# Second half of an adaLN modulation: from TensorE in the projection stage to GpSimd in the attention stage

## The chip, the cores and the metric

The kernel runs on one core of a Trainium2 chip. The metric is the device time of one execution in microseconds (us). Five engines take part, each with its own queue of instructions that it works off in order: PE (matmuls, with PEld for its weight loads), DVE (VectorE), ACT (ScalarE), POOL (GpSimd) and SP, whose queue issues nearly all DMAs. An instruction that waits holds up everything behind it on its engine.

## The reference, cut to what matters

A transformer block on 2048 tokens of width 448, all in fp32: the conditioning vector `c` gives six rows of modulation, then attention with 16 heads of 28, then an MLP of width 1792.

```python
mod = (silu(c) @ w_mod).reshape(1, 6, 1, 448)
sa, ca, ga, sb, cb, gb = (mod[:, i] for i in range(6))
h = layernorm(x) * (1 + ca) + sa
x = x + ga * attention(h, wqkv, wo)          # softmax over all 2048 keys
h = layernorm(x) * (1 + cb) + sb
x = x + gb * mlp(layernorm(h), w1, b1, w2, b2)   # gelu
```

`sa` and `ca` are needed at once. `ga`, `sb`, `cb` and `gb` come into play late: `ga` is multiplied into the rows of `wo`, `gb` into `w2` and `b2`, `sb` and `cb` make the input of the MLP.

## The kernel before, in words

The work has three stages, and all of its order is written out by hand: each engine's queue is the order in which the Python code emits instructions.

**Projection (0 to 166 us).** The tokens are in four blocks `b` of 512. For each block a list of tasks is run through, numbered `n`: products of queries or keys for one group of four heads (`qk_task`), products of values (`v_task`). A task is 11 matmuls into a PSUM tile `pa`. Between tasks PE is given maxima: the softmax needs the maximum of each query's scores, and it is found ahead by a product of one key chunk with one query chunk into a PSUM tile of a ring of five (`ma`, `ma`, `m`, `m`, `m`; line 476) and a reduction by DVE into a small tile `mxp` (line 481). Some maxima go in pairs: ACT takes the relu of a difference (L489), DVE finishes it in a custom instruction (L493). Into the first four tasks of block 1 the second part of the modulation is put, `mod_mm(0)` to `mod_mm(3)`: each multiplies `silu(c)` (128 x 32 weights, `sil_b`) with 128 rows of `w_mod` (1792 columns, loaded by `mod_load` into `slot_v`) in four matmuls that write 32 partitions each of one tile `o` (L752). `mod_fin` copies the sums out with ACT, writes them to DRAM (`drow`) and reads each of the four rows back, spread over 128 partitions.

**Attention (166 to 794 us).** 16 units (four groups of heads times four query blocks), 16 steps each, 256 steps. In a step PE makes the scores of one key chunk for four heads in two halves (L1382, tiles `s`), ACT takes their exponential (L1395), and PE multiplies those of the step before with the values (L1337, tile `o`). Maxima for later units are put between. Up to step 120 three PSUM tiles (`m`) are there for them; from step 121 (`RING`) one of these banks becomes a third `s` tile, a single tile `m` is left for single maxima, and maxima in pairs go into the `s` tile that is free just then (L686). At the end of a unit `unit_end_tasks` divides by the softmax sums: a reciprocal on DVE, a trip through DRAM that spreads it, a product on POOL (`t_split`, L1062), a rounding to fp32r on DVE (`t_split2`, L1072), the remainder on POOL (L1073), and eight DMAs that store both. `max_fin` gathers a unit's maxima into a tile `m32`, whose unused half POOL zeroes each time (L517). Tasks that belong to a certain step are put into a table by `at(step, fn)` and run at the end of that step. So is the preparation of `wo` (five items: a product with `ga` on POOL, a rounding on DVE, L987, a remainder on POOL), from step 4 on.

**Projection by `wo` and MLP.** Units 12 and 13 (steps 216 to 219 and 232 to 235) hold the output projection of the first two query blocks, which needs `wo`. The MLP follows after step 255, 794 to 1097 us.

The tiles `slot_a2h`, `slot_a3h` and `slot_b1h` belong to weights and inputs in the projection stage. In the attention stage `b1h` is used in step 0, and all three take outputs of attention from step 205 on.

Of the kernel before, what the change touches and what calls it, by code (L numbers as in the profile page):

```python
# [22 lines left out]
D = 448  # L23
# [21 lines left out]
def tile_adaln_block(ctx: ExitStack, tc: tile.TileContext, x, wqkv, wo, w1, b1, w2, b2, c, w_mod, out):  # L45
# [75 lines left out]

    ident = sbt("ident", [128, 128])
    make_identity(nc, ident)
    cst = sbt("cst", [128, 5])
    neg_half, zero_col = cst[:, 0:4], cst[:, 4:5]
    pool.memset(neg_half, -0.5)
    pool.memset(zero_col, 0.0)


    cols = sbt("cols", [128, 2 * NC])  # L130
# [183 lines left out]
    pc = ps_o()  # L314
    pe.transpose(pc[:, :NC], c_rows, ident[:NC, :NC])
    act.activation(sil_b, pc[:, :NC, None].broadcast_to([128, NC, 32]), AF.Silu)
    warm_up(5)
    for k in range(NC):
        for j in range(2):
# [190 lines left out]
            at(clock[0] + 4, lambda: make_kd(g))  # L510

    late = []


    def max_fin(g, qt):
# [223 lines left out]

    mod = {}  # L740

    def mod_load(k):
        mod[k] = slot(f"v{2 + k % 2}", [128, 4 * D], F32)
        load_mod(mod[k], k, 2 * D, 4)

    def mod_mm(k):
        if k == 0:
            mod["p"] = ps_o()
        p = mod["p"]
        for j in range(4):  # L750
            rs_, cs = mod_part(k, j, 4)
            pe.matmul(  # L752
                p[32 * j : 32 * j + 32, :D], sil_b[rs_, k, :], mod[k][rs_, cs],
                start=(k == 0), stop=(k == NC - 1),
            )

    def mod_fin():
        t = sbt("full", [128, 512], bufs=3)
        act.copy(t[0:64, :D], mod["p"][0:64, :D])
        act.activation(t[64:96, :D], mod["p"][64:96, :D], AF.Identity, bias=1.0)  # L760
        act.copy(t[96:128, :D], mod["p"][96:128, :D])
# [56 lines left out]
    for b in range(NB):  # L818
# [12 lines left out]
        for n, (tb, kind, g) in enumerate(tasks):  # L831
# [130 lines left out]
    def wo_item(n):  # L962
# [11 lines left out]
        def go(r):  # L974
            full = sbt("full", [128, 512], bufs=3)
            ps = slice(0, 112 if n == 3 else 128)
            pool.tensor_tensor(out=full[ps, :D], in0=r[ps, :D], in1=rows["ga"][ps], op=ALU.mult)

            def rest():
                if n == 3:  # L980
                    hi = sbt("hi", [128, 512], F32R, bufs=3)
                    dve.tensor_copy(hi[ps, :D], full[ps, :D])
                    pool.tensor_tensor(out=wo_p[1][ps, 2, :], in0=full[ps, :D], in1=f(hi)[ps, :D], op=ALU.subtract)
                    pool.tensor_copy(wo_p[1][0:32, 2, :], f(hi)[0:32, :D])
                    return
                k = min(n, 3)
                dve.tensor_copy(wo_p[0][:, k, :], full[:, :D])  # L987
# [3 lines left out]
            at(6 + 2 * n, rest)  # L991

        return ld, go

# [44 lines left out]
    def unit_end_tasks(u, o_sb):  # L1039
# [24 lines left out]
        def t_split2():  # L1064
# [7 lines left out]
            (dve.tensor_copy if staged else act.copy)(hi, on)  # L1072
# [179 lines left out]
        sched.setdefault(step, []).append(fn)  # L1252

    wo_prep = Prep([wo_item(n) for n in range(5)])
    at(0, lambda: wo_prep.load(2))
    for n in range(5):
        at(4 + 2 * n, wo_prep.step)

    def b2_load():
        rows["b2"] = raw_t()  # L1260
# [13 lines left out]
        at(1 + i, lambda: put_spare(1))  # L1274
    for g in (1, 2):
        at(6 + g, lambda g=g: put_ones(g))
    at(15, b2_load)
    at(28, b2_mul)
    last0 = NKT * (NU - 1)
    lnst = [ln2_stages(b) for b in range(NB)]  # L1280
    for i in range(14):
# [259 lines left out]
```

## Time and profile before

| | |
|---|---|
| median of 3 runs | 1099.84 us (1099.55 to 1100.01) |
| profiled execution | 1099.75 us, span 1097.5 us |
| busy in the span | PE 1088.1 us, DVE 805.1, ACT 697.6, POOL 198.7 |
| granted TensorE clock | 1.00 throughout |
| HBM | 59.39 MB read, 29.50 MB written |

The span begins with the first instruction that was recorded; 2.25 us of the execution lie outside of it. In the timeline a row is one or more instructions of one line in a row: start, duration of the whole row, engine, line, operation, tiles written and read, shape, count, and in brackets the engine's idle time before it with what ended it. Matmuls overlap in PE's pipeline, so that a row of several is shorter than their sum; PEld rows mark the moments at which PE took up a matmul.

### The profile page before, as it was taken

How to read it: one execution, taken by the hardware profiler on the slowest of the kernel's cores; microseconds unless marked ns; L12 is line 12 of the kernel's file. 1: busy time of each engine (PE TensorE's matmuls, PEld its weight loads, DVE VectorE, ACT ScalarE, POOL GpSimd, SP SyncE). 2: the span in 40 equal slices, each digit the busy share in tenths (PEclk: the TensorE clock that was granted, in tenths of full speed). 3: DMA queues.
4: the chain of work that ended last, by engine and by line, in shares of the span. 5: the costliest groups of instructions: out<-in, count | busy, mean ns of one | idle time of the engine just before them, and what ended most of it. 6: DMA issues, size and time to landing. Idle time of an engine off the chain costs nothing.

```text
span 1097.5 us, 20709 instructions
## 1 busy us (share of the span) xinstructions
PE 1088.1 (99%) x8255; PEld 658.3 (60%) x8255; DVE 805.1 (73%) x1382; ACT 697.6 (64%) x883; POOL 198.7 (18%) x201
## 2 busy tenths in 40 slices
PE   8999999999999999999999999999999999999998
PEld 6756675444444444444444444554488788888887
DVE  6968788999999999988888888575655565463322
ACT  4565667888888888888888888678933411211211
POOL 1543332210000000000000000217123042061000
PEclk9999999999999999999999999999999999999999
DMA  9563354121222201232211213111442302002000
GB/s 312 207 190 103 97 188 134 59 65 32 72 76 64 77 28 41 67 98 54 69 48 38 86 49 104 58 31 59 136 137 65 101 34 55 18 34 72 34 1 34
DMA packets 58438, 88.57 MB, mean 81 GB/s; under 512 B 13759, under 2 KB 25686, under 8 KB 58330
## 3 DMA queue, kind: packets, MB, share of 16 engines
q1 hardware_dynamic: 57858, 86.51, 26.3%
q8 instruction: 65, 1.06, 0.4%
q10 hardware_dynamic: 148, 0.46, 0.1%
q0 software_dynamic: 336, 0.28, 0.1%
q14 instruction: 31, 0.25, 0.1%
HBM read 59.39 MB, written 29.50 MB: 81 GB/s over the span
## 4 chain that ended last, share of the span: by engine, by line
PE 96%; DVE 2%; DMA 1%; ACT 1%; issue 0%; SPq 0%; DVEq 0%; ACTq 0%
PE s L1382 23%; PE o L1337 23%; PE m L396 16%; PE pa L396 9%; PE m L476 8%; PE s L1472 3%; PE s L1473 3%; PE s L1474 3%; PE s L476 2%; PE t L1473 1%; PE t L1474 1%; PE t L1472 1%; DVE y L1193 1%; DMA slot_c<-in_w_mod_dram 1%; PE o L277 1%; DVE mxp L481 0%
## 5 line engine op out<-in xcount | busy, mean ns | idle before, releaser
L481 DVE TENSOR_REDUCE mxp<-m 128x1 f32<-128x512 f32 x555 | 359.7, 685 | 65.0 <-PE m L476 49.6
L1382 PE MATMUL s<-slot_b,slot_a 28*128 28x512 f32 (+1 forms) x3072 | 356.7, 423 | 0.0
L1382 PEld LDWEIGHTS s<-slot_b,slot_a 28*128 28x128 f32 (+1 forms) x3072 | 211.1, 183 | 176.0 <-ACT slot_c L1395 96.4
L476 PE MATMUL m<-kh,qh 28*128 28x512 f32 x607 | 226.9, 468 | 0.5 <-DVE mxp L481 0.3
L1395 ACT ACTIVATE slot_c<-s 128x1024 f32<-128x1024 f32 x170 | 174.7, 1028 | 51.6 <-PE s L1382 50.8
L1337 PE MATMUL o<-slot_c,v 128*32 128x512 f32 x680 | 178.9, 605 | 0.0
L1428 ACT ACTIVATE full<-m,b_col 128x512 f32<-128x512 f32 x56 | 38.6, 689 | 206.6 <-PE m L396 201.4
L686 DVE TENSOR_REDUCE mxp<-s 128x2 f32<-128x1024 f32 x107 | 131.1, 1226 | 5.1
L1337 PE MATMUL o<-slot_c1h,v 128*32 128x512 f32 x512 | 134.7, 605 | 0.0
L1337 PE MATMUL o<-slot_c0h,v 128*32 128x512 f32 x508 | 133.6, 605 | 0.0
L1395 ACT ACTIVATE slot_c1h<-s 128x1024 f32<-128x1024 f32 x128 | 130.7, 1021 | 0.0
L1395 ACT ACTIVATE slot_c0h<-s 128x1024 f32<-128x1024 f32 x127 | 130.5, 1028 | 0.0
L1395 ACT ACTIVATE slot_d<-s 128x1024 f32<-128x1024 f32 x86 | 88.4, 1028 | 25.0 <-PE s L1382 24.7
L1431 DVE CAST hi<-full 128x512 fp32r<-128x512 f32 x42 | 18.7, 444 | 112.3 <-ACT full L1428 112.3
L476 PEld LDWEIGHTS m<-kh,qh 28*128 28x128 f32 x607 | 90.7, 182 | 15.2 <-DVE mxp L481 13.1
L1337 PE MATMUL o<-slot_d,v 128*32 128x512 f32 x344 | 90.5, 605 | 0.4 <-ACT osb L1301 0.4
L1062 POOL TENSOR_TENSOR osb<-osb,osb 128x512 f32<-128x512 f32 x16 | 20.6, 1286 | 362.8 <-DMA osb<-drec 343.5
L1432 DVE TENSOR_TENSOR lo<-full,hi 128x512 fp32r<-128x512 f32 x56 | 46.0, 822 | 29.7 <-ACT hi L1431 25.1
L396 PE MATMUL m<-y,slot_a 128*128 128x512 f32 x160 | 60.9, 397 | 0.4 <-DVE y L1193 0.2
L481 DVE TENSOR_REDUCE mxp<-ma 128x1 f32<-128x512 f32 x61 | 39.5, 681 | 13.2 <-PE m L476 9.2
L1337 PEld LDWEIGHTS o<-slot_c,v 128*32 128x32 f32 x680 | 24.5, 108 | 39.1 <-issue 36.5
L650 DVE CUSTOM_DVE_ANT_0 slot_d0i<-m,slot_d0i 128x512 f32<-128x512 f32 x54 | 37.3, 691 | 14.3 <-PE m L476 11.3
(351 smaller groups left out, 1824.2 us busy)
## 6 DMA issues: line engine op xcount, KB each, us to landing
slot_b<-d SPq DMA_DIRECT2D x32, 256.0 KB
slot_a<-d SPq DMA_DIRECT2D x32, 256.0 KB
d<-lo SPq DMA_DIRECT2D x28, 256.0 KB
d<-hi SPq DMA_DIRECT2D x16, 256.0 KB
osb<-drec SPq DMA_DIRECT2D x15, 256.0 KB
out_dram<-xn SPq DMA_DIRECT2D x16, 224.0 KB
raw<-in_B_w_dram SPq DMA_DIRECT2D x14, 224.0 KB
qh<-d SPq DMA_DIRECT2D x12, 256.0 KB
```

Of the source, the lines that this page charges most:

```text
L396: pe.matmul(p, a, b, start=(i == 0), stop=(i == len(terms) - 1))
L476: pe.matmul(m, qh_sb[(g, qt)][js, i * 128 : (i + 1) * 128], k[js, :], start=True, stop=True)
L481: dve.tensor_reduce(out=mxp[(g, qt)][:, i, j, cch : cch + 1], in_=m, op=ALU.max, axis=AX.X)
L686: dve.tensor_reduce(out=mxp[(g, qt)][:, i, j : j + 2, cch], in_=t, op=ALU.max, axis=AX.X)
L1337: pe.matmul(o[32 * j : 32 * j + 32, :], v_sb[kt // 4][:, kt % 4, 4 * g + j, :], p[j // 2][:, j % 2, :], start=(kt == 0), stop=(kt == NKT - 1),
L1382: pe.matmul(s2[:, jj, :], ks[rows_, kp, kc], qs[rows_, qp, :], start=(term == 0), stop=(term == 2))
L1395: act.activation(pt[hf], s2, AF.Exp, scale=SCALE)
L1428: act.activation(gf, p, AF.Gelu_apprx_tanh, bias=b1_col[:, i : i + 1])
L1432: dve.tensor_tensor(out=glo, in0=gf, in1=f(ghi), op=ALU.subtract)
L1472: pe.matmul(pp, ghi[:, ts], w_hi, start=(m == 0), stop=False)
L1473: pe.matmul(pp, ghi[:, ts], w_lo, start=False, stop=False)
L1474: pe.matmul(pp, glo[:, ts], w_hi, start=False, stop=(m == NFT - 1))
```

## The change

Three things are done at once.

1. The second part of the modulation leaves PE and the projection stage. ACT makes `sil_c` (128 x 4) at the start. In steps 124 to 161 of attention, every fifth step, one chunk of `w_mod` (128 rows, or for the last of each half 64, by 896 columns) is loaded into `slot_a2h`; two steps later POOL multiplies it with a column of `sil_c` and adds it to a running sum (`slot_b1h` for `ga` and `sb`, `slot_a3h` for `cb` and `gb`). In step 166 four matmuls with a column of ones as weights (one that `v_sb` holds already) sum over the partitions, into the single tile `m`; one ACT instruction copies the result, with a bias column `third` that adds the 1 of `cb`.
2. With it, the preparation of `wo` moves from steps 4 to 14 to steps 178 to 188, the load of `b2` from 15 to 189 and its product from 28 to 202.
3. The rounding in `t_split2` goes to POOL where results are stored (units 0 to 11 and 14), and `m32` becomes two fixed tiles that are zeroed once.

The diff, without the constants' other uses:

```diff
+MOD_AT = 124
+WO_AT = 178
...
+    act.activation(sil_c, pc[:, :NC], AF.Silu)
...
-        m32 = sbt("m32", [128, 32], F32R, bufs=2)
-        pool.memset(f(m32)[:, 16:32], 0.0)
+        m32s.append(m32s.pop(0))
+        m32 = m32s[-1]
...
-    def mod_load(k):
-        mod[k] = slot(f"v{2 + k % 2}", [128, 4 * D], F32)
-        load_mod(mod[k], k, 2 * D, 4)
-
-    def mod_mm(k):
-        if k == 0:
-            mod["p"] = ps_o()
-        p = mod["p"]
+    def mod_load(h, k):
+        rs_ = mod_rows(h, k)
+        mod["raw"] = slot("a2h", [128, 2 * D], F32)
+        c0 = 2 * D * (1 + h)
+        sp.dma_start(mod["raw"][rs_], w_mod[128 * k : min(128 * k + 128, D), c0 : c0 + 2 * D])
+
+    def mod_add(h, k):
+        rs_ = mod_rows(h, k)
+        if k == 0:
+            mod[h] = slot(("b1h", "a3h")[h], [128, 2 * D], F32)
+        raw, total = mod["raw"][rs_], mod[h][rs_]
+        col = sil_c[rs_, k : k + 1].broadcast_to([rs_.stop - rs_.start, 2 * D])
+        pool.tensor_tensor(out=raw if k else total, in0=raw, in1=col, op=ALU.mult)
+        if k:
+            pool.tensor_tensor(out=total, in0=total, in1=raw, op=ALU.add)
+
+    def mod_fin():
+        p = ps_mx()
+        ones_ = v_sb[0].rearrange("p t h d -> p (t h) d")[:, 0:32, DH]
         for j in range(4):
-            rs_, cs = mod_part(k, j, 4)
             pe.matmul(
-                p[32 * j : 32 * j + 32, :D], sil_b[rs_, k, :], mod[k][rs_, cs],
-                start=(k == 0), stop=(k == NC - 1),
+                p[32 * j : 32 * j + 32, :D], ones_, mod[j // 2][:, j % 2 * D : (j % 2 + 1) * D], start=True, stop=True,
             )
-
-    def mod_fin():
         t = sbt("full", [128, 512], bufs=3)
-        act.copy(t[0:64, :D], mod["p"][0:64, :D])
-        act.activation(t[64:96, :D], mod["p"][64:96, :D], AF.Identity, bias=1.0)
-        act.copy(t[96:128, :D], mod["p"][96:128, :D])
+        act.activation(t[:, :D], p[:, :D], AF.Identity, bias=third)
...
-            if b == 0 and n == 6:
-                mod_load(0)
-                mod_load(1)
-            if b == 1:
-                if n < 2:
-                    mod_mm(n)
-                    mod_load(2 + n)
-                elif n in (2, 3):
-                    mod_mm(n)
-                    if n == 3:
-                        mod_fin()
...
-            (dve.tensor_copy if staged else act.copy)(hi, on)
+            (pool.tensor_copy if staged else act.copy)(hi, on)
...
-    at(0, lambda: wo_prep.load(2))
+    for i in range(2 * NC):
+        h, k = divmod(i, NC)
+        at(MOD_AT + 5 * i, lambda h=h, k=k: mod_load(h, k))
+        at(MOD_AT + 5 * i + 2, lambda h=h, k=k: mod_add(h, k))
+    at(MOD_AT + 10 * NC + 2, mod_fin)
+    at(WO_AT - 4, lambda: wo_prep.load(2))
     for n in range(5):
-        at(4 + 2 * n, wo_prep.step)
+        at(WO_AT + 2 * n, wo_prep.step)
```

PE's order at the end of the third task of block 1, in the kernel before (`ma` and `m` are the ring of tiles for maxima, `slot_v` holds `w_mod`, `pa` is the next task's tile):

```order
L476 MATMUL ma_847<-kh_162_730,qh_60_323 128x512
L476 MATMUL m_191_850<-kh_162_730,qh_60_323 128x512
L476 MATMUL m_192_853<-kh_162_730,qh_60_323 128x512
L476 MATMUL m_193_856<-kh_74_361,qh_158_708 128x512
L752 MATMUL o_761<-slot_v_172_766,slot_d_4_86 32x448 x4
L396 MATMUL pa_876<-slot_c_110_510,slot_a_20_125 128x512
L396 MATMUL pa_876<-slot_c_110_510,slot_a_22_127 128x512
```

The same place in the changed kernel:

```order
L481 MATMUL ma_836<-kh_163_733,qh_63_330 128x512
L481 MATMUL m_189_839<-kh_163_733,qh_63_330 128x512
L481 MATMUL m_190_842<-kh_163_733,qh_63_330 128x512
L481 MATMUL m_191_845<-kh_77_368,qh_159_711 128x512
L401 MATMUL pa_861<-slot_c_113_517,slot_a_21_127 128x512
L401 MATMUL pa_861<-slot_c_113_517,slot_a_23_129 128x512
```

The four matmuls of the modulation are gone from between the maxima and the next task, here and at three other places; nothing else on PE changes place there.

PE's order at the end of step 166 in the changed kernel (`o` is the product with the values, `s` the scores, `m` the one tile for single maxima):

```order
L1346 MATMUL o_7761<-slot_d_1901_7896,v_233 32x512 x2
L772 MATMUL m_1913_7954<-slot_b1h_6662,v_232 32x448 x2
L772 MATMUL m_1913_7954<-slot_a3h_7316,v_232 32x448 x2
L1391 MATMUL s_1921_7972<-slot_b_1766_7276,slot_a_1581_6427 128x512 x2
L481 MATMUL m_1922_7975<-kh_1814_7482,qh_1394_5669 128x512
L1391 MATMUL s_1921_7972<-slot_b_1766_7276,slot_a_1581_6427 128x512 x4
```

The four new matmuls stand between the values of one step and the scores of the next, and the next single maximum, two matmuls later, writes the same PSUM bank.

POOL's order in units 7 to 9 in the changed kernel (`slot_a2h` holds a chunk of `w_mod`, `osb` the output of a unit):

```order
L764 TENSOR_TENSOR slot_a2h_6925<-slot_a2h_6925,sil_c_86 128x896
L766 TENSOR_TENSOR slot_b1h_6662<-slot_b1h_6662,slot_a2h_6925 128x896
L1066 TENSOR_TENSOR osb_6865<-osb_6725,osb_6865 128x512
L1076 CAST hi_7079<-osb_6865 128x512
L1077 TENSOR_TENSOR lo_7080<-osb_6865,hi_7079 128x512
L764 TENSOR_TENSOR slot_a2h_7077<-slot_a2h_7077,sil_c_86 64x896
L766 TENSOR_TENSOR slot_b1h_6662<-slot_b1h_6662,slot_a2h_7077 64x896
```

And POOL's order for three such units in the kernel before:

```order
L1062 TENSOR_TENSOR osb_6418<-osb_6255,osb_6418 128x512
L1073 TENSOR_TENSOR lo_6653<-osb_6418,hi_6652 128x512
L517 MEMSET m_1700_6923 128x16
L1062 TENSOR_TENSOR osb_6952<-osb_6814,osb_6952 128x512
L1073 TENSOR_TENSOR lo_7161<-osb_6952,hi_7160 128x512
L517 MEMSET m_1838_7555 128x16
```

A unit's product, rounding and remainder now stand together on POOL, with products and sums of the modulation before and behind them; the memsets are gone.

More of the change, by code (lines that the diff above doesn't have):

```diff
@@ L123, in tile_adaln_block @@
     make_identity(nc, ident)
-    cst = sbt("cst", [128, 5])
-    neg_half, zero_col = cst[:, 0:4], cst[:, 4:5]
+    cst = sbt("cst", [128, 6])
+    neg_half, zero_col, third = cst[:, 0:4], cst[:, 4:5], cst[:, 5:6]
     pool.memset(neg_half, -0.5)
-    pool.memset(zero_col, 0.0)
+    pool.memset(cst[:, 4:6], 0.0)
+    pool.memset(third[64:96], 1.0)
+    sil_c = sbt("sil_c", [128, NC])
     cols = sbt("cols", [128, 2 * NC])
@@ L512, in tile_adaln_block @@
     late = []
+    m32s = [sbt(f"m32_{i}", [128, 32], F32R) for i in range(2)]
+    for m32 in m32s:
+        pool.memset(f(m32)[:, 16:32], 0.0)
     def max_fin(g, qt):
-        m32 = sbt("m32", [128, 32], F32R, bufs=2)
-        pool.memset(f(m32)[:, 16:32], 0.0)
+        m32s.append(m32s.pop(0))
+        m32 = m32s[-1]
         dve.tensor_reduce(
@@ L740, in tile_adaln_block, with mod_rows @@
     mod = {}
-    def mod_load(k):
-        mod[k] = slot(f"v{2 + k % 2}", [128, 4 * D], F32)
-        load_mod(mod[k], k, 2 * D, 4)
-    def mod_mm(k):
-        if k == 0:
-            mod["p"] = ps_o()
-        p = mod["p"]
+    def mod_rows(h, k):
+        return slice(0, 128) if k < 3 else slice(64 * h, 64 * h + 64)
+    def mod_load(h, k):
[5 more added lines that the diff above has]
+        rs_ = mod_rows(h, k)
+        if k == 0:
+            mod[h] = slot(("b1h", "a3h")[h], [128, 2 * D], F32)
[7 more added lines that the diff above has]
+        ones_ = v_sb[0].rearrange("p t h d -> p (t h) d")[:, 0:32, DH]
         for j in range(4):
-            rs_, cs = mod_part(k, j, 4)
             pe.matmul(
-                p[32 * j : 32 * j + 32, :D], sil_b[rs_, k, :], mod[k][rs_, cs],
-                start=(k == 0), stop=(k == NC - 1),
+                p[32 * j : 32 * j + 32, :D], ones_, mod[j // 2][:, j % 2 * D : (j % 2 + 1) * D], start=True, stop=True,
             )
-    def mod_fin():
         t = sbt("full", [128, 512], bufs=3)
-        act.copy(t[0:64, :D], mod["p"][0:64, :D])
-        act.activation(t[64:96, :D], mod["p"][64:96, :D], AF.Identity, bias=1.0)
-        act.copy(t[96:128, :D], mod["p"][96:128, :D])
+        act.activation(t[:, :D], p[:, :D], AF.Identity, bias=third)
         sp.dma_start(drow, t[0:128:32, :D])
@@ L989, in rest @@
                     pool.tensor_tensor(out=wo_p[1][:, k, :], in0=full[:, :D], in1=f(wo_p[0])[:, k, :], op=ALU.subtract)
-            at(6 + 2 * n, rest)
+            at(WO_AT + 2 + 2 * n, rest)
         return ld, go
@@ L1276, in tile_adaln_block @@
         at(6 + g, lambda g=g: put_ones(g))
-    at(15, b2_load)
-    at(28, b2_mul)
+    at(WO_AT + 11, b2_load)
+    at(WO_AT + 24, b2_mul)
     last0 = NKT * (NU - 1)
```

## The prediction

> **What bounds the kernel now.** I read the chain of waits on the page first, then busy time by stretches, then the timeline at the three places that the change touches.
>
> ```profile
> PE 96%; DVE 2%; DMA 1%; ACT 1%; issue 0%; SPq 0%; DVEq 0%; ACTq 0%
> 57.30:75.50 18.20, 18.20 (x98) 9.83 (x97) 11.06 (x21) 11.15 (x22) 5.49 (x6) 1.00 0.67 210
> 205.00:452.00 247.00, 247.00 (x2368) 116.04 (x2362) 225.64 (x421) 212.43 (x248) 20.65 (x24) 1.00 0.20 57
> 490.00:634.00 144.00, 144.00 (x1480) 62.25 (x1476) 125.14 (x147) 125.92 (x133) 10.45 (x11) 1.00 0.22 62
> ```
>
> The columns behind a stretch are its length and the busy times of PE, PEld, DVE, ACT and POOL, then the granted clock, the DMA share and GB/s. PE has no gap in the tasks from which the modulation goes (first stretch), nor in attention. DVE follows: 91% in the attention before `RING`, 87% behind it, so that single DVE instructions can still hold PE up there. POOL has 93% of its time free behind `RING`. So the change is worth what it takes from PE's queue, less what it puts back there, plus what DVE's relief ends in short stalls.
>
> **The matmuls that go.**
>
> ```profile
> 57.34 0.16 PEld L752 LDWEIGHTS o<-slot_v,slot_d 128*32 128x32 f32 x8 [0.35 <-issue]
> 58.23 0.76 PEld L396 LDWEIGHTS pa<-slot_c,slot_a 128*128 128x128 f32 x4 [0.73 <-ACT full L432]
> 71.89 0.15 PEld L752 LDWEIGHTS o<-slot_v,slot_d 64*32 64x32 f32 x8 [0.24 <-issue]
> 72.78 0.77 PEld L396 LDWEIGHTS pa<-slot_c,slot_a 128*128 128x128 f32 x4 [0.73 <-ACT full L432]
> ```
>
> First and last of four: from the take-up of a `mod_mm` to that of the next task is 0.89 us, so 4 x 0.89 = 3.56 us leave PE. What can be late instead is DVE. In the fourth task it works off nine maxima almost without a pause:
>
> ```profile
> 66.66 0.69 DVE L481 TENSOR_REDUCE mxp<-ma 128x1 f32<-128x512 f32 x1 [2.25 <-PE m L476]
> 67.27 1.28 DVE L481 TENSOR_REDUCE mxp<-m 128x1 f32<-128x512 f32 x2
> 68.99 0.18 PEld L476 LDWEIGHTS ma<-kh,qh 28*128 28x128 f32 x2 [0.36 <-ACT xn L234]
> 69.53 1.29 DVE L481 TENSOR_REDUCE mxp<-ma 128x1 f32<-128x512 f32 x2 [0.38 <-PE m L476]
> 71.47 0.18 PEld L476 LDWEIGHTS m<-kh,qh 28*128 28x128 f32 x1 [0.28 <-DVE mxp L481]
> 76.11 0.69 DVE L481 TENSOR_REDUCE mxp<-m 128x1 f32<-128x512 f32 x1 [2.29 <-PE ma L476]
> ```
>
> Without the third `mod_mm` PE comes to the four maxima of 68.99 at 68.10, while the fourth tile of the ring is read until 67.27 + 1.28 = 68.55: about 0.3 us lost. The group behind them already waited for DVE at 71.47 and comes earlier again; DVE can only make up its pause of 0.38, so I take 0.2 there. Before the next group DVE rested 2.29 us, which absorbs the rest. Term one: -3.56 + 0.5 = -3.06 us; bounds -3.56 (no stall) and -1.78 (both later `mod_mm` turn into waits for DVE).
>
> With them go three ACT copies, 3.2 MB of loads and SP's issues. PE waits for none of these in the first stretch, where ACT is busy 11.15 of 18.20 us: nothing. `sil_c` and the new memsets run at the start, while weights are awaited: nothing.
>
> **The matmuls that come, step 166.** They are shaped like one `mod_mm`: +0.89 us. Then the handover of the single tile `m`, read off a step of the same kind:
>
> ```profile
> 562.39 0.11 PEld L1337 LDWEIGHTS o<-slot_c,v 128*32 128x32 f32 x2 [0.28 <-ACT osb L1301]
> 563.12 1.06 ACT L1395 ACTIVATE slot_c1h<-s 128x1024 f32<-128x1024 f32 x1
> 563.38 0.18 PEld L1382 LDWEIGHTS s<-slot_b,slot_a 29*128 29x128 f32 x2 [0.84 <-ACT slot_c L1395]
> 563.39 0.50 PE L476 MATMUL m<-kh,qh 28*128 28x512 f32 x1
> 563.72 0.74 PE L1382 MATMUL s<-slot_b,slot_a 28*128 28x512 f32 x8
> 563.96 0.69 DVE L481 TENSOR_REDUCE mxp<-m 128x1 f32<-128x512 f32 x1 [0.16 <-PE m L476]
> 566.96 0.11 PEld L1337 LDWEIGHTS o<-slot_d,v 128*32 128x32 f32 x2 [0.36 <-issue]
> 74.57 0.53 ACT L761 COPY full<-o 32x448 f32<-32x448 f32 x1
> ```
>
> The step's second exponential ends at 564.18, 0.80 us behind the take-up of the next scores; put back by 0.89, that take-up finds ACT free. A reader follows PE by 0.07 us (563.39 + 0.50 to 563.96), the copy takes 0.53, so the next maximum can start 0.6 to 0.7 us behind its place. Two score matmuls go ahead of it; those behind it normally start 0.34 us after the first (563.38 to 563.72). PE loses some 0.4 us, and scores, exponentials and all later work queue behind. Term two: +0.89 + 0.4 = +1.3 us; bounds 0.9 (no stall) and 2.2 (the copy is caught behind a whole exponential of 1.06 too and a second step is hit).
>
> **The sums on POOL.**
>
> ```profile
> L1265 POOL TENSOR_TENSOR row_b2g<-raw,row_gb 128x448 f32<-128x448 f32 x1 | 1.2, 1157 | 0.0
> L1062 POOL TENSOR_TENSOR osb<-osb,osb 128x512 f32<-128x512 f32 x16 | 20.6, 1286 | 362.8 <-DMA osb<-drec 343.5 <-ACT slot_d L1395 19.4
> L984 POOL CAST slot_e<-hi 32x448 fp32r<-32x448 f32 x1 | 0.5, 546 | 0.1
> 61.04 0.42 SPq L161 DMA_DIRECT2D slot_v<-in_w_mod_dram  x1
> 66.75 0.16 PEld L752 LDWEIGHTS o<-slot_v,slot_d 128*32 128x32 f32 x8 [0.37 <-DMA slot_v<-in_w_mod_dram]
> ```
>
> From 448 to 512 elements a product grows by 0.129 us, so 896 should take about 1.157 + 7 x 0.129 = 2.06 us. A chunk of 448 KB lands within the 5.7 us that its predecessor of 896 KB took (61.04 to 66.75). A chunk then needs at most 5.7 + 2 x 2.06 = 9.8 us of its five steps, which last 5 x 2.29 = 11.4 us (two steps from 562.39 to 566.96). The last is loaded in step 159, added by 164, used in 166. PE does not wait; on SP a load waits at most briefly for the one raw tile, ahead of loads that have steps to spare. Nothing.
>
> **The rounding that leaves DVE.** It stands ahead of maxima on DVE at the end of every unit. Two steps without it (unit 0), then with it (first and last of six units):
>
> ```profile
> 196.85 0.11 PEld L1337 LDWEIGHTS o<-slot_c,v 128*32 128x32 f32 x2 [0.37 <-issue]
> 201.80 0.11 PEld L1337 LDWEIGHTS o<-slot_d,v 128*32 128x32 f32 x2 [0.36 <-issue]
> 236.91 0.11 PEld L1337 LDWEIGHTS o<-slot_c,v 128*32 128x32 f32 x2 [0.36 <-issue]
> 238.26 0.42 DVE L1072 CAST hi<-osb 128x512 fp32r<-128x512 f32 x1
> 242.16 0.11 PEld L1337 LDWEIGHTS o<-slot_c,v 128*32 128x32 f32 x2 [0.37 <-issue]
> 437.38 0.11 PEld L1337 LDWEIGHTS o<-slot_c,v 128*32 128x32 f32 x2 [0.37 <-issue]
> 442.40 0.11 PEld L1337 LDWEIGHTS o<-slot_d,v 128*32 128x32 f32 x2 [0.36 <-issue]
> ```
>
> 4.95 us against 5.25 in unit 1 and 5.02 in unit 6; the six are over by 0.30, 0.25, 0.08, 0.02, 0.13 and 0.07, 0.85 in all. A memset of `mxp` shares the first two, and the steps behind give a little back: I take -0.65 us, bounds -0.9 and 0. Behind `RING` the same steps show no stall, so no gain. On POOL it takes about 0.6 us (0.55 for 32 rows), right behind the product, with time to spare. Taking the memset of `m32` from POOL keeps DVE from waiting behind the sums: it prevents a cost.
>
> **The preparation of `wo`, moved.** `wo` is needed in step 216 and ready by 190. Its five roundings meet a DVE that rests 0.16 us ahead of a single maximum in a step, and the wait for pairs is bounded by a third `s` tile.
>
> ```profile
> L987 DVE CAST slot_e<-full x4: 381/382/383, 185.8 to 205.9; 128x448 fp32r<-128x448 f32 x4
> 777.53 1.29 POOL L1062 TENSOR_TENSOR osb<-osb,osb 128x512 f32<-128x512 f32 x1 [12.67 <-DMA osb<-drec]
> 777.98 1.12 DVE L1221 CAST slot_b<-raw 128x512 fp32r<-128x512 f32 x1 [1.09 <-DMA raw<-in_B_w_dram]
> 779.75 0.42 DVE L1221 CAST slot_b<-raw 128x512 fp32r<-128x512 f32 x1
> 680.35 1.28 POOL L1062 TENSOR_TENSOR osb<-osb,osb 128x512 f32<-128x512 f32 x1 [20.68 <-DMA osb<-drec]
> 680.83 0.69 DVE L481 TENSOR_REDUCE mxp<-m 128x1 f32<-128x512 f32 x1 [0.24 <-PE m L476]
> ```
>
> All roundings of `wo` took 0.38 us beside the same POOL products: free in unit 0 to within 0.1, and as much in unit 11. Net 0; bounds -0.1 and +0.9. The upper one is for POOL in the way: a rounding from SBUF beside a POOL product took 1.12 us for 0.42, 0.7 more, while a maximum, which reads PSUM, kept its 0.69. Five such, 3.5 us of DVE, of which the rests take most.
>
> The Trainium skill (GPSIMD Engine Reference, section 1, Specifications) has the two engines share their SBUF interfaces, with contention for DVE instructions in a two-port mode or with two SBUF inputs. The pair of 777.98 and 779.75 agrees. By that rule the upper bound is the likely value for the roundings, and the sum would be 0.9 us higher; by the rows of L987 it stays, and I go by these.
>
> **Sum.** -3.06 + 1.3 - 0.65 + 0 = -2.4 us on the profiled 1099.75 (span 1097.5 and 2.25 outside), so 1097.3. The profile lies 0.1 us under the median of 1099.84, which the sum ignores.
>
> **The rivals.**
>
> *DVE and the one tile take back more.* Both later `mod_mm` become waits (-1.78) and the handover costs its bound (2.2), with the roundings at half (-0.3): +0.1; midway to the forecast 1098.6. For it: DVE's nine maxima in a row. Against: DVE is busy 11.06 of 18.20 us there.
>
> *DVE's relief is worth more.* No stall in projection, handover hidden, all 0.85 saved: -3.56 + 0.89 - 0.85 = -3.5, so 1096.2. Against: a ring of five tiles and one tile are short buffers.
>
> *The roundings of `wo` are held by POOL.* Each meets a product, now that unit 10's own three POOL instructions fall into the same steps: the upper bound of +0.9, so 1098.2. For it: the row at 777.98. Against: L987's narrow 381 to 383 ns. It is the rule cited above at work.
>
> *PE waits for POOL in step 166*, the slower side. One raw tile means that loads and sums alternate: 8 x 5.7 + 14 x 2.06 + 6.4 for two units' own work = 80.8 us, with 42 x 2.29 = 96.2 to go. It decides from (96.2 + 2.4 - 52.0) / 14 = 3.3 us an instruction; at 3.6 PE waits 6.2 us in front of everything, 1103.5. For it: no row has a broadcast column or 896 elements. Against: every POOL product keeps to 2.0 ns an element.
>
> **How the numbers follow.** Forecast 0.68, its own range 1096.6 to 1098.1; more taken back 0.13; more gained 0.06; roundings held 0.07; slower 0.06. A measurement here can tell about 0.2%, 2.2 us, from no change, so faster begins at 1097.6. Of the forecast's 0.68 I put 0.51 under that and 0.17 above; with the 0.06, faster is 0.57; with 0.13 and 0.07, same is 0.37; slower 0.06. The range takes in all cases but the last: 1096.1 to 1098.9.
>
> **What would show it.** Right: the four tasks of block 1 shorter by 0.89, 0.89 and together 1.3 us; unit 10 longer by 1.3 with one step of some 3.6 us; two steps of 4.95 to 5.0 in units 1 to 6; L764 and L766 at 2.1 us. Wrong: PE waiting for POOL at L772, or DVE casts near 1.1 us in unit 11.

## The result, and the profile after

| | before | after |
|---|---|---|
| median of 11 runs each | 1100.01 us (1099.41 to 1101.55) | 1097.67 us (1096.95 to 1099.22) |
| profiled execution, span | 1099.75 us, 1097.5 us | 1098.11 us, 1096.3 us |
| busy: PE, DVE, ACT, POOL | 1088.1, 805.1, 697.6, 198.7 us | 1087.1, 802.4, 696.6, 232.6 us |

The ratio is 0.9978, 95% interval 0.997 to 0.9986: faster by 2.3 us, in the range of the forecast (1097.3, 1096.1 to 1098.9). The two profiled executions lie only 1.6 us apart, their spans 1.2; why is told below.

The chain of waits of the changed kernel, and two stretches (length, then busy times of PE, PEld, DVE, ACT and POOL, granted clock, DMA share, GB/s):

```profile
PE 97%; DVE 2%; ACT 1%; issue 0%; DMA 0%; ACTq 0%; DVEq 0%
56.70:71.70 15.00, 15.00 (x68) 9.61 (x67) 10.81 (x20) 9.33 (x20) 6.48 (x6) 1.00 0.48 178
490.00:634.00 144.00, 143.57 (x1464) 61.88 (x1460) 124.08 (x145) 124.83 (x133) 47.76 (x36) 1.00 0.33 93
```

PE is still the bound. POOL's busy time in the last stretch rose from 10.45 to 47.76 us, and PE there has 0.43 us in which it does nothing, where it had none before: the sums are hidden, but not everything that came with them.

Where the difference lies is read off the moments at which PE takes up the first value matmuls of each unit, in both traces. First the two ends of the projection stage, in the kernel before and in the changed one:

```profile
14.92 1.00 PEld L802 LDWEIGHTS pa<-slot_b,slot_a 128*128 128x128 f32 x5 [0.32 <-DVE slot_b L301]
171.68 0.11 PEld L1337 LDWEIGHTS o<-slot_d,v 128*32 128x32 f32 x2 [0.27 <-issue]
```

```profile
15.51 1.00 PEld L817 LDWEIGHTS pa<-slot_b,slot_a 128*128 128x128 f32 x5 [0.32 <-DVE slot_b L305]
168.64 0.11 PEld L1346 LDWEIGHTS o<-slot_d,v 128*32 128x32 f32 x2 [0.27 <-issue]
```

From 156.76 to 153.13 us: 3.63 less. The start itself is 0.59 us later, and that is not the change. In `cast_alone` below, which has the program of before up to there, the same row stands at 16.33:

```profile
16.33 1.00 PEld L802 LDWEIGHTS pa<-slot_b,slot_a 128*128 128x128 f32 x5 [0.32 <-DVE slot_b L301]
```

So the start differs by 1.4 us between two executions of the same instructions, more than half of what the change is worth. `single_late` and `wo_later`, which are alike up to there and ran on one chip, differ by 0.94 (14.67 and 15.61). The table therefore leaves the start out. Each number is the length of a stretch, less its length before, in us; a unit reaches from its first step's take-up of value matmuls to the next unit's. There is one profile of each kernel.

| kernel | projection | units 1 to 6 | unit 10 | unit 11 |
|---|---|---|---|---|
| after | -3.63 | -0.45 | +1.51 | +0.68 |
| `cast_alone` | +0.16 | -0.50 | 0.00 | -0.01 |
| `wo_alone` | -0.07 | +0.13 | -0.01 | +0.78 |
| `no_matmuls` | -3.60 | -0.24 | +0.02 | +0.01 |
| `single_late` | -3.62 | -0.38 | +1.36 | -0.01 |
| `wo_later` | -3.67 | -0.37 | +1.49 | -0.01 |
| `both` | -3.69 | -0.50 | +1.31 | 0.00 |
| `cast_back` | -3.65 | +0.11 | +1.53 | +0.48 |
| `memsets_back` | -3.47 | -0.42 | +1.54 | +0.55 |
| `sums_twice` | -3.56 | -0.43 | +2.09 | +0.07 |

Units 7 to 9 and 13 to 15 differ by under 0.1 us in all of them. Where nothing was changed, longer stretches differ by up to 0.16 (the projection of `cast_alone`, units 1 to 6 of `wo_alone`): smaller differences say nothing. In the changed kernel unit 12 gives back 0.12, and the stretch behind the last value matmul is 0.13 longer. With the start: +0.59 - 3.63 - 0.45 + 1.51 + 0.68 - 0.12 + 0.13, and +0.07 from the other units, is -1.2 us, the difference of the spans. Without the start it is -1.8, and without the 0.68 of unit 11, which not all profiles have, -2.5, by the median's -2.3.

Step 166 of the changed kernel, PE's take-ups and what ACT does for the single tile `m`:

```profile
570.22 0.11 PEld L1346 LDWEIGHTS o<-slot_c1h,v 128*32 128x32 f32 x2 [0.36 <-issue]
571.11 0.17 PEld L772 LDWEIGHTS m<-slot_b1h,v 128*32 128x32 f32 x2 [0.25 <-issue]
571.97 0.18 PEld L1391 LDWEIGHTS s<-slot_b,slot_a 29*128 29x128 f32 x2 [0.67 <-ACT slot_c0h L1404]
572.11 0.63 ACT L776 ACTIVATE full<-m,cst 128x448 f32<-128x448 f32 x1 [0.21 <-PE m L772]
572.79 0.18 PEld L481 LDWEIGHTS m<-kh,qh 28*128 28x128 f32 x1 [0.64 <-ACT full L776]
573.91 0.11 PEld L1346 LDWEIGHTS o<-slot_c,v 128*32 128x32 f32 x2 [0.36 <-issue]
```

The step takes 3.69 us (570.22 to 573.91). The matmuls at L772 wait for nothing but issue. Then PE's weight loads stand for 0.64 us at the next maximum until ACT has read `m`, with the other scores behind it.

The roundings: the two steps of unit 1 that took 5.25 us (236.91 to 242.16) now take 4.98. Those of unit 6, 5.02 before (437.38 to 442.40), take 5.00 (last two rows):

```profile
233.96 0.11 PEld L1346 LDWEIGHTS o<-slot_c,v 128*32 128x32 f32 x2 [0.36 <-issue]
238.94 0.11 PEld L1346 LDWEIGHTS o<-slot_c,v 128*32 128x32 f32 x2 [0.37 <-issue]
433.94 0.11 PEld L1346 LDWEIGHTS o<-slot_c,v 128*32 128x32 f32 x2 [0.37 <-issue]
438.94 0.11 PEld L1346 LDWEIGHTS o<-slot_d,v 128*32 128x32 f32 x2 [0.36 <-issue]
```

And unit 11, steps 186 to 188, POOL and DVE and one take-up of PE:

```profile
616.87 1.15 POOL L981 TENSOR_TENSOR full<-raw,row_b2g 128x448 f32<-128x448 f32 x1 [5.31 <-DMA raw<-in_A_wo_dram]
617.81 0.46 DVE L986 CAST hi<-full 112x448 fp32r<-112x448 f32 x1
617.97 1.45 POOL L1066 TENSOR_TENSOR osb<-osb,osb 128x512 f32<-128x512 f32 x1
621.09 0.61 POOL L1076 CAST hi<-osb 128x512 fp32r<-128x512 f32 x1
621.78 1.29 POOL L1077 TENSOR_TENSOR lo<-osb,hi 128x512 fp32r<-128x512 f32 x1
622.26 1.05 DVE L991 CAST slot_e<-full 128x448 fp32r<-128x448 f32 x1
625.37 0.18 PEld L1391 LDWEIGHTS s<-slot_b,slot_a 29*128 29x128 f32 x2 [0.55 <-DVE mxp L693]
```

The fifth and last rounding of `wo` starts beside POOL's remainder for unit 10 (621.78 to 623.07) and ends just behind it, after 1.05 us in place of 0.38. DVE's maxima behind it are late, and PE's weight loads wait 0.55 us for one of them.

### The profile page after: what moved, and what is told of

It reads as the page before. It is cut to its first block, busy times and chain, and to the rows that moved or that the text cites. A ratio compares the mean times of both kernels' runs of the same rounds, so it can differ in the third digit from the quotient of the medians.

```text
span 1096.3 us, 20660 instructions
## 1 busy us (share of the span) xinstructions
PE 1087.1 (99%) x8231; PEld 659.9 (60%) x8231; DVE 802.4 (73%) x1369; ACT 696.6 (64%) x882; POOL 232.6 (21%) x215
## 3 DMA queue, kind: packets, MB, share of 16 engines
q8 instruction: 64, 1.05, 0.4%
## 4 chain that ended last, share of the span: by engine, by line
PE 97%; DVE 2%; ACT 1%; issue 0%; DMA 0%; ACTq 0%; DVEq 0%
PE s L1391 23%; PE o L1346 23%; PE m L401 16%; PE pa L401 9%; PE m L481 8%; PE s L1481 3%; PE s L1482 3%; PE s L1483 3%; PE s L481 2%; PE t L1482 1%; PE t L1483 1%; PE t L1481 1%; DVE y L1197 1%; PE o L281 1%; PE ma L481 0%
```

## The experiments

The theory after the two traces: three terms of the prediction at other sizes (projection, step 166, roundings), and one of its rivals, the roundings of `wo` held by POOL, at work on one rounding. The rival for each term is that something else in the change made the difference.

**The roundings alone** (`cast_alone`: before, with one edit).

```diff
-            (dve.tensor_copy if staged else act.copy)(hi, on)
+            (pool.tensor_copy if staged else act.copy)(hi, on)
```

> The kernel before, with one edit: the rounding of stored results goes from DVE to POOL; the memset of m32 stays on POOL, modulation and wo as before. Theory of the prediction, as the trace of the changed kernel corrects it: units 1 to 6 shorter by about 0.45 us in all (the changed kernel has -0.23, -0.12, -0.01, -0.11, 0 and 0), nothing elsewhere, so 1099.4 us. Rival (in the changed kernel the saving is cut by what else moved): the whole excess of 0.85 us goes, units 1 and 2 shorter by 0.30 and 0.25. Second rival: the memset of m32, now behind the rounding on POOL, holds the finished maxima up, and the units gain nothing.

Units 1 to 6 are shorter by 0.50 us, unit 1 by 0.30 and unit 4 by 0.13 of it. So the rest of the change does not cut the saving, the memset of `m32` does not undo it, and the whole 0.85 does not come. Of the pairs of steps from which the prediction read the 0.85, only that of unit 1 gave way, from 5.25 to 4.98 us. Those of units 2 to 6 took 5.20, 5.03, 4.97, 5.08 and 5.02 us before and 5.17, 5.03, 5.02, 5.08 and 5.01 here. In unit 2 the step with the rounding gained 0.23 and the next lost 0.21; in unit 5 neither moved. The other 0.2 us came in small amounts in other steps of units 2 and 4. The time was 1100.34 beside 1100.87 us, one run each.

**The rounding back on DVE** (`cast_back`: the changed kernel, with that line undone).

> The changed kernel, with the rounding of stored results back on DVE. Units 1 to 6 should get back the 0.46 us they gained. In units 7 to 10 the sums of the modulation now follow each unit's product on POOL: if a DVE rounding beside a POOL product is held to that product's end, one or more of these roundings takes 0.9 to 2.1 us in place of 0.42, and a step of units 8 to 10 is longer by some tenths. Rival (a rounding is as quick beside POOL, and the 0.69 us seen at step 188 had another cause): all of them at 0.42 and units 7 to 10 as in the changed kernel.

Units 1 to 6 lose the gain (+0.11). None of the roundings in units 7 to 10 started beside a sum, so that they could not decide between theory and rival: twelve of the thirteen kept their 0.42 us. The one for unit 10 started beside a POOL cast of 32 rows (620.98 to 621.53) and took 0.47, to 621.81. The 0.48 of unit 11 is a rounding of `wo` again, now the fourth, beside POOL's product for unit 10:

```profile
617.03 1.16 POOL L981 TENSOR_TENSOR full<-raw,row_b2g 128x448 f32<-128x448 f32 x1 [4.72 <-DMA raw<-in_A_wo_dram]
618.15 1.29 POOL L1066 TENSOR_TENSOR osb<-osb,osb 128x512 f32<-128x512 f32 x1
618.58 1.11 DVE L986 CAST hi<-full 112x448 fp32r<-112x448 f32 x1
```

**Without the four matmuls** (`no_matmuls`: the sums over the partitions, and with them the second part of the modulation, are left out).

```diff
-        p = ps_mx()
...
-        for j in range(4):
-            pe.matmul(
-                p[32 * j : 32 * j + 32, :D], ones_, mod[j // 2][:, j % 2 * D : (j % 2 + 1) * D], start=True, stop=True,
-            )
...
-        act.activation(t[:, :D], p[:, :D], AF.Identity, bias=third)
+        act.activation(t[:, :D], mod[0][:, :D], AF.Identity, bias=third)
```

> The changed kernel without the four matmuls of step 166: the activation that follows reads one half's sums from SBUF instead, so the result of the modulation's second part is left out; loads, sums on POOL and the rows' way through DRAM stay. If the 1.5 us by which unit 10 grew are these matmuls and the handover of the single tile, unit 10 comes back to its length before, and step 166 from 3.69 to about 2.2 us. Rival (the sums on POOL, their loads or the rows' DMAs slow the unit): some of the 1.5 us stays. A split: 0.89 is the matmuls' own time, 0.6 the handover.

```profile
570.57 0.11 PEld L1340 LDWEIGHTS o<-slot_c1h,v 128*32 128x32 f32 x2 [0.36 <-issue]
571.57 0.18 PEld L1385 LDWEIGHTS s<-slot_b,slot_a 29*128 29x128 f32 x2 [0.84 <-ACT slot_c L1398]
572.72 0.11 PEld L1340 LDWEIGHTS o<-slot_c,v 128*32 128x32 f32 x2 [0.25 <-issue]
```

PE's take-ups: the step is back at 2.15 us, unit 10 at its old length. The 1.5 us are the matmuls and the handover. The two can be told apart: from the take-up of the values to that of the scores it is 1.00 us here and 1.75 in the changed kernel (570.22 to 571.97), so 0.75 is the matmuls' and the other 0.8 the handover's. Sums, loads, the rows' way through DRAM and ACT's copy itself cost PE nothing.

**The single maximum later** (`single_late`).

```diff
-            late_one, after = after, more
+            late_one, after = after or step == MOD_AT + 10 * NC + 3, more
```

> The changed kernel, with the single maximum of step 167 put behind the fourth pair of score matmuls of its step instead of behind the first, so that the activation reading m has 0.7 us more before m is written again. Theory: PE's wait for that activation (0.3 to 0.6 us at the maximum, and what it delays) goes, unit 10 longer than before by 0.9 to 1.0 instead of 1.51. Rival: the wait only moves, to the reader of the late maximum, and unit 10 stays 1.3 to 1.5 longer.

```profile
572.01 0.18 PEld L481 LDWEIGHTS m<-kh,qh 28*128 28x128 f32 x1 [0.30 <-ACT full L776]
614.60 1.16 POOL L981 TENSOR_TENSOR full<-raw,row_b2g 128x448 f32<-128x448 f32 x1 [4.02 <-DMA raw<-in_A_wo_dram]
615.72 1.28 POOL L1066 TENSOR_TENSOR osb<-osb,osb 128x512 f32<-128x512 f32 x1
616.81 0.45 DVE L986 CAST hi<-full 112x448 fp32r<-112x448 f32 x1
```

The wait for ACT fell from 0.64 to 0.30 us, unit 10 from +1.51 to +1.36: less than the theory's 0.5 to 0.6, nearer to the rival. PE reaches the later place sooner than ACT is done. What I had not foreseen is unit 11: +0.68 is gone, although `wo` stands where it stood. In this execution POOL waited 4.02 us for the last load of `wo`, not 5.31. The fourth rounding met only the last 0.19 us of POOL's product for unit 10, and the fifth met nothing.

**The preparation of `wo` ten steps later** (`wo_later`).

```diff
-WO_AT = 178
+WO_AT = 188
```

> The changed kernel, with the preparation of wo ten steps later (188 to 198 instead of 178 to 188), so that its five roundings on DVE lie between unit 10's product and subtraction on POOL (steps 186 and 187) and unit 11's (202 and 203). Theory: the 0.69 us that step 188 lost in the changed kernel came from one rounding held by POOL's subtraction for unit 10 (1.05 us for 0.4), so unit 11 goes back to its length before, within 0.15, and every rounding takes 0.38 to 0.47. Rival: the roundings of wo cost by their place among DVE's maxima or by POOL's own products for wo; then one or more of them is still near 1.0 us, and unit 11 or 12 longer by some 0.7.

```profile
L991 DVE CAST slot_e<-full 128x448 fp32r<-128x448 f32 x4 | 1.5, 383 | 0.0
```

Unit 11 at -0.01, the groups of DVE with all roundings at 0.33 to 0.38 us: as the theory had it. Since executions with 178 can be free of the loss too, this run alone would not decide.

**`wo` moved alone** (`wo_alone`: before, with only the steps of `wo` and `b2` changed as in the change).

```diff
-    at(0, lambda: wo_prep.load(2))
+    at(174, lambda: wo_prep.load(2))
...
-        at(4 + 2 * n, wo_prep.step)
+        at(178 + 2 * n, wo_prep.step)
```

> The kernel before, in which only the preparation of wo goes to steps 178 to 188 (and the loads and product of b2 behind it); modulation and roundings of stored results as before. Theory: what it costs depends on when the last load of wo lands: POOL's wait ahead of the last product at 4.0 to 4.1 us goes with no loss, 4.7 to 4.8 with a rounding of 1.1 us and 0.5 us in step 186, 5.3 with 0.7 in step 188; unit 0 gains nothing. Rival (the move is free by itself, and costs only beside the other two changes): no rounding of wo over 0.5 us and unit 11 within 0.1 us, whatever that wait.

```profile
618.20 1.19 POOL L977 TENSOR_TENSOR full<-raw,row_b2g 128x448 f32<-128x448 f32 x1 [4.99 <-DMA raw<-in_A_wo_dram]
619.34 1.30 POOL L1062 TENSOR_TENSOR osb<-osb,osb 128x512 f32<-128x512 f32 x1
619.47 1.42 DVE L982 CAST hi<-full 112x448 fp32r<-112x448 f32 x1
```

The move costs by itself: 1.42 us for a rounding that took 0.33 in `wo_later`, and unit 11 longer by 0.78. The seven profiles with `wo` at 178 order themselves by POOL's wait for that load, as expected:

| POOL's wait for the last load of `wo` | kernel | longest rounding of `wo` | unit 11 |
|---|---|---|---|
| 4.02, 4.04 us | `single_late`, `no_matmuls` | 0.45, 0.42 us | -0.01, +0.01 us |
| 4.31 | `sums_twice` | 0.68 | +0.07 |
| 4.72, 4.80 | `cast_back`, `memsets_back` | 1.11, 1.19 | +0.48, +0.55 |
| 4.99 | `wo_alone` | 1.42 | +0.78 |
| 5.31 | after | 1.05 (the fifth; the fourth took 0.46) | +0.68 |

POOL's product for unit 10 follows on that of the last load, while the fourth rounding comes from DVE's own order. In all seven the fourth rounding starts during a POOL product and ends 0.25 us behind it; how long it takes depends on how much of the product is left. That is 0.19 us in `single_late` (616.81 to 617.00) and 1.17 in `wo_alone` (619.47 to 620.64). In the changed kernel the rounding starts 0.16 us ahead of unit 10's product, so that only 0.21 us of the product before it is left; it takes 0.46, unit 10's product 1.45 in place of 1.28, and the fifth rounding meets the remainder. Two DMAs differ between the profiles. SP issues the last load behind unit 10's `osb<-drec`, which is issued 3.17 us behind the store it needs in `single_late` and 3.63 in the changed kernel (3.2 to 4.0 over the seven); from the load's first issue to POOL's product it is 6.00 and 6.89 us. Why these DMAs differ stays open.

**POOL beside every rounding** (`meet_sum`, `meet_copy`, `meet_none`: `wo_later`, with POOL let go just ahead of each rounding; in `meet_none` POOL's line is left out).

```diff
             def rest():
...
+                dve.memset(dummy[:, 0:1], 0.0)
+                pool.tensor_tensor(out=dummy, in0=dummy, in1=dummy, op=ALU.mult)   # meet_copy: pool.tensor_copy(dummy, dummy)
+                for _ in range(3):
+                    dve.memset(small, 0.0)
```

> The kernel with the preparation of wo at 188 (no rounding of wo met POOL there), with one added product on POOL, of a spare tile of 128x448 by itself (1.15 us), let go by a tiny memset on DVE 0.1 to 0.2 us ahead of each of the five roundings of wo. Theory: a DVE rounding that starts beside a POOL product ends with it, so all five take 0.9 to 1.2 us in place of 0.33 to 0.38, and each costs PE some 0.3 to 0.7 us as the single collisions did (0.48 to 0.69): units 11 and 12 longer by 1.5 to 3 us together. Rival (the long roundings were late for another reason, such as the landing of a load): the roundings stay at 0.4 and the units are longer only by the tiny memsets, under 0.5 us in all.

> As the run with the added products, but what POOL does beside each rounding is a copy of the same tile (one input from SBUF, 0.5 to 0.6 us). If only a product with two inputs keeps DVE from SBUF, the roundings stay near 0.4 us and the units within 0.5 us; if any POOL instruction does, they end with the copy, at 0.5 to 0.7 us, and the units are longer by some 0.3 us more than the tiny memsets cost.

> As the runs with an added product or copy on POOL beside each rounding of wo, with the four tiny memsets on DVE ahead of each rounding, but nothing added on POOL. It splits the 3.2 and 1.2 us by which units 10 to 12 grew in those two, beyond the four matmuls of step 166. Theory: the roundings take 0.33 to 0.38 us again, and the memsets alone cost under 0.5 us, so that holding the roundings by 0.3 us (copy) cost about 0.8 and by 0.7 us (product) about 2.8. Rival: the memsets' order on DVE is what cost, and about 1 us stays.

The first rounding in `meet_sum`, then in `meet_copy`, then in `meet_none`:

```profile
626.76 0.93 POOL L989 TENSOR_TENSOR slot_a2h<-slot_a2h 128x448 f32<-128x448 f32 x1 [8.65 <-DVE slot_a2h L991]
626.87 1.07 DVE L999 CAST slot_e<-full 128x448 fp32r<-128x448 f32 x1
```

```profile
626.15 0.55 POOL L989 COPY slot_a2h<-slot_a2h 128x448 f32<-128x448 f32 x1 [8.74 <-DVE slot_a2h L991]
626.28 0.68 DVE L999 CAST slot_e<-full 128x448 fp32r<-128x448 f32 x1
```

```profile
627.35 0.39 DVE L998 CAST slot_e<-full 128x448 fp32r<-128x448 f32 x1
```

A rounding ends 0.25 us behind POOL's instruction, whether that has two inputs or one (627.94 behind 627.69; 626.96 behind 626.70), in all five cases of each of the two runs: 1.07 and 0.68 us, against 0.39 with nothing beside it. Units 11 and 12 together are longer by 3.22, 1.24 and 0.30 us. So five roundings held by 0.68 us cost PE 2.92 us, 0.58 each, and held by 0.28 us 0.94, 0.19 each: most of a hold reaches PE, as DVE has few rests here. It reaches PE by DVE's maxima: in units 11 and 12 PE's weight loads for scores wait for a maximum five times, 3.0 us in all, in `meet_sum`, and four times, 0.8 us, in `meet_copy`. The rival of `meet_copy`, that only two inputs hold a rounding, has fallen.

**The memsets of `m32` back on POOL** (`memsets_back`).

```diff
-        m32s.append(m32s.pop(0))
-        m32 = m32s[-1]
+        m32 = sbt("m32", [128, 32], F32R, bufs=2)
+        pool.memset(f(m32)[:, 16:32], 0.0)
```

> The changed kernel, with the zeros of m32 written by POOL anew for every finished maximum, as before, not once at the start. If the fixed tiles prevent a cost, as the prediction says, the reduction on DVE that fills m32 waits at least once in units 7 to 10 for a memset that stands behind sums on POOL, up to 3.8 us (1.68 + 2.11 for one chunk), and DVE's maxima behind it and then PE are late by 1 to 3 us. Rival (POOL is idle two thirds of that time and the memsets fall into the gaps): no change, all units within 0.1 us.

```profile
L522 DVE TENSOR_REDUCE m<-mxp 128x16 fp32r<-128x64 f32 x16 | 3.5, 220 | 0.6
```

The groups of DVE: all sixteen reductions into `m32` (`m` in this row) together had 0.6 us of idle time ahead of them. Units 7 to 9 are as in the changed kernel to 0.05 us. The rival holds: the fixed tiles prevent nothing here.

**Every product and sum twice** (`sums_twice`).

```diff
-        pool.tensor_tensor(out=raw if k else total, in0=raw, in1=col, op=ALU.mult)
+        for _ in range(2):
+            pool.tensor_tensor(out=raw if k else total, in0=raw, in1=col, op=ALU.mult)
         if k:
-            pool.tensor_tensor(out=total, in0=total, in1=raw, op=ALU.add)
+            for _ in range(2):
+                pool.tensor_tensor(out=total, in0=total, in1=raw, op=ALU.add)
```

> The changed kernel with every product and every sum of the modulation issued twice on POOL (the second part of the modulation comes out wrong). A chunk then takes 4.7 us of loading and 2 x (1.68 + 2.11) = 7.6 us of POOL, 12.3 us against five steps of 11.4, so the sums run behind their plan: the last would end some 9 us later than the 557.9 of the changed kernel, 567, still ahead of step 166 (571). Theory: PE does not wait, every unit as in the changed kernel within 0.1 us, so the sums lie hidden even at twice their price. Rival (the margin is smaller than it looks, as loads queue on SP and units' own work stands between): PE waits at the four matmuls for POOL, by 1 to 6 us, and the time rises as much.

```profile
567.12 4.28 POOL L768 TENSOR_TENSOR slot_a3h<-slot_a3h,slot_a2h 64x896 f32<-64x896 f32 x2
571.45 0.21 PEld L774 LDWEIGHTS m<-slot_a3h,v 128*32 128x32 f32 x4 [0.40 <-POOL slot_a3h L768]
```

The last sum ended at 571.40, not 567, and PE waited for it at the second half's matmuls; unit 10 grew by a further 0.58 us. The theory's "PE does not wait" was wrong by a little, the rival's 1 to 6 us by more: twice the price is just where the margin ends.

**Both mends** (`both`: `single_late` and `wo_later` together).

> The changed kernel with both mends: the single maximum of step 167 put later in its step, and the preparation of wo ten steps later. By the two profiles apart: 0.15 us from the first; from the second 0.69 in those executions in which a rounding of wo meets POOL's subtraction, nothing in the others. So 0.2 to 0.8 us under the changed kernel, and against before a ratio of 0.9972 to 0.9978; a gain that five rounds may not tell from the changed kernel's own 0.9978.

1097.40 us (1096.66 to 1097.98, 8 runs) against 1100.29 of before; ratio 0.9974, interval 0.9964 to 0.9985. Its trace is the best of all those with the whole computation in the table's terms (1.31, 0.00), but the interval overlaps that of the changed kernel: not told apart by time.

## Why the prediction was right, and where not

**The bound** held: what PE's queue lost and got back is the result.

**Term one, the matmuls that go: -3.06 forecast, -3.5 to -3.7 measured** in the eight kernels of the table that have this edit. The step that failed is the price of 0.89 us from take-up to take-up. It leaves out the idle time of the weight loads ahead of the `mod_mm`, 0.35 us at the first one (57.34). Around it, PE's weight loads of the task before, in the kernel before and in the changed one:

```profile
56.57 0.41 PEld L396 LDWEIGHTS pa<-slot_c0h,slot_a 128*128 128x128 f32 x2
```

```profile
57.09 0.41 PEld L401 LDWEIGHTS pa<-slot_c0h,slot_a 128*128 128x128 f32 x2
57.54 0.87 PEld L401 LDWEIGHTS pa<-slot_c,slot_a 128*128 128x128 f32 x4
67.11 0.18 PEld L481 LDWEIGHTS m<-kh,qh 28*128 28x128 f32 x1 [0.32 <-DVE mxp L486]
69.12 0.18 PEld L481 LDWEIGHTS m<-raw,qh 28*128 28x128 f32 x1 [0.36 <-DVE mxp L486]
69.52 0.18 PEld L481 LDWEIGHTS m<-kh,qh 28*128 28x128 f32 x1 [0.21 <-DVE mxp L486]
69.95 0.75 PEld L401 LDWEIGHTS pa<-slot_c,slot_a 128*128 128x128 f32 x4 [0.25 <-issue]
```

From these loads to the next task's take-up it was 1.66 us (56.57 to 58.23) and is now 0.45: 1.21 saved, of which 0.12 comes back within the task. Ahead of each of the other three `mod_mm` stands a group of maxima. There the idle time stays and now stands ahead of the next task (0.24 us ahead of the last `mod_mm` at 71.89, 0.25 ahead of the task at 69.95), and the second and third gave 0.9 each. The stall on DVE came where the prediction put it, in the fourth task: 0.48 us, forecast 0.5, but all of it at the first group of maxima (67.11) and none at the second. The last `mod_mm` gave 0.94, and some 0.2 more came in small steps by the end of the stage. The stall was right, the price was not.

**Term two, step 166: +1.3 forecast, +1.51 measured.** One long step came as told (3.69 us, forecast 3.6), but both of its parts had another size. The matmuls cost 0.75, not 0.89. The handover cost 0.8 in place of 0.4. ACT's copy with a bias column took 0.63 us, not the 0.53 of the 32-row copy I had taken it from, so that the maximum was taken up 0.82 us behind the first scores (571.97 to 572.79), not 0.6 to 0.7. And nearly all of this was lost: the 0.3 us that the prediction took off, since two score matmuls go ahead of the maximum, were not saved.

**The sums on POOL: nothing forecast, nothing measured.** Products took 1.68 us and sums 2.11, where 2.06 was the estimate:

```profile
L764 POOL TENSOR_TENSOR slot_a2h<-slot_a2h,sil_c 128x896 f32<-128x896 f32 x4 | 6.7, 1682 | 36.4 <-DMA slot_a2h<-in_w_mod_dram 36.3
L766 POOL TENSOR_TENSOR slot_b1h<-slot_b1h,slot_a2h 128x896 f32<-128x896 f32 x2 | 4.2, 2112 | 0.2
```

The rival's point of decision, 3.3 us an instruction, was too low: `sums_twice` has (16 x 1.68 + 12 x 2.11) / 14 = 3.73 in place of each, for which the prediction's sum gives 8 us of waiting (45.6 + 52.2 + 6.4 = 104.2 us, with 96.2 to go), and PE lost 0.58. The sum had 5.7 us for a load. In the changed kernel it was 3.4 to 6.3 us from issue to POOL's start, 4.6 in the mean of the six loads that POOL waited for, which makes the sum 95 us. The view of the tile `slot_a2h` from 480 us on (shortest, median and longest in ns, then the first and the last start: 483.6 to 488.3 and 550.6 to 554.1):

```profile
L756 SPq DMA_DIRECT2D slot_a2h<-in_w_mod_dram x7: 333/416/541, 483.6 to 550.6; - x7
L764 POOL TENSOR_TENSOR slot_a2h<-slot_a2h,sil_c x6: 1674/1682/1682, 488.3 to 554.1; 128x896 f32<-128x896 f32 x4, 64x896 f32<-64x896 f32 x2
```

**The roundings: -0.65 forecast, -0.45 measured** (-0.24 to -0.50 over the kernels). The step that failed is the 0.85: the prediction put all by which six pairs of steps stood over unit 0's 4.95 down to the rounding. Unit 1's pair lost its excess without it (0.27 of 0.30); those of units 2 to 6 kept theirs, 0.55 in all, to within 0.05 each, in `cast_alone` and in the changed kernel. What makes those five pairs longer stays open. That the fixed tiles for `m32` prevent a cost has fallen.

**`wo` moved: 0 forecast, 0 to +0.78 measured.** The step that failed is "as much in unit 11": in unit 0 the roundings never started beside a POOL product, which their narrow 381 to 383 ns showed only for that place. The rival "roundings held by POOL" was the mechanism at work, on one rounding of five and with a price of 0.5 to 0.8 us in four of seven profiles. The Trainium skill (SBUF — State Buffer, section "Who interferes with whom") counts casts among the DVE operations that can take the port pair shared with GpSimd, lets whichever starts first have it for its whole instruction, and says that `tensor_reduce` never contends on this chip. The runs agree: roundings end just behind POOL's instruction (1.07 and 0.68 us for 0.39), a POOL product that starts behind a rounding is longer (1.45 us for 1.28, at 617.97), and the maxima beside POOL kept their 0.69.

**The sum.** -2.4 forecast and -2.3 by the medians is partly luck: 0.5 us more from the projection stage against 0.2 less from step 166, 0.2 less from the roundings, and a held rounding in some executions. The median, 1097.67 us, lies at the 1097.6 from which the forecast counted the change as faster, so this result does not tell its chances for faster and same apart. Of the signs named, the long step, the 2.11 us of a sum and the absence of a wait at L772 for POOL came. The products took 1.68, not 2.1; the first task was shorter by 1.1, not 0.89; of the pairs of steps only unit 1's came down, to 4.98. The sign for "wrong", a DVE cast near 1.1 us in unit 11, came too.

Left open: the 0.13 to 0.27 us by which the end behind the last value matmul is longer in the kernels with the modulation on POOL (0.02 and -0.06 in the two without), and the start.

## What to carry to other kernels

Price a group of matmuls that is to go from the take-up of what stands ahead of it to the take-up of what stands behind it, and look at the idle time ahead of it: here 0.3 us went with the group where nothing else stood between the matmuls around it, and stayed where maxima did. Before work is moved to an "idle" time, look for the other engine whose instructions can be held there, and check the starts, not the averages: here a cast on DVE that began during a POOL product ended 0.25 us behind it. Before an excess is put down to one instruction, take that instruction away: five of six pairs of steps kept theirs. An effect of 0.1% is read by stages of the trace, with the start left out, since the start alone differed by 1.8 us between executions.

## What the runs showed of the hardware

A DVE rounding from SBUF that starts during a POOL instruction ends 0.25 us behind it, for a copy with one input (0.55 us) as for a product (0.93 us); tiny memsets (0.06 us) and maxima from PSUM (0.69) that started during POOL instructions were not held. Nor was, in the projection stage of both kernels, a cast of 128x512 that started during a POOL instruction on 128x4 elements: it took 0.42 us and ended 0.53 ahead of it (27.07 in the kernel before). A POOL product of 1.28 us that started 0.16 us behind a rounding took 1.45. A POOL product with a broadcast column as its second input took 1.68 us for 896 elements, a sum of two full tiles 2.11. The moment of PE's first projection matmul lay between 14.53 and 16.33 us over the twelve experiments and the two kernels.
